# A chunk's last head pair placed behind its search, MLP steps over two ticks fewer, first products sorted

## The chip, the cores and the metric

The kernel runs on one NeuronCore of one Trainium2 chip, in one launch. Its engines are TensorE (PE; its weight loads are shown as PEld), VectorE (DVE), ScalarE (ACT), GpSimd (POOL) and SyncE (SP), which issues every DMA here. The metric is the device time of one execution in microseconds. Three runs of the kernel before gave 1281.82, 1284.70 and 1287.45 us.

## The reference

```python
# q, k, v: (4, 8, 576, 64)
scores = q @ k.T / 8
kth = the 32nd largest score of each row of 576
attn = softmax over the scores >= kth (the rest is masked)
x = (attn @ v) as 2304 tokens x 512
h = x @ w_in;  g = h - tanh(h);  x = g @ w_out           # MLP 0: 512 -> 2048 -> 512
h = x @ w_in;  g = h if h > 0 else exp(h) - 1;  out = g @ w_out   # MLP 1
```

All inputs are fp32.

## The kernel before, in words

The 2304 tokens are cut into six chunks of 384 rows (`CHUNKS`), numbered 0 to 5. A chunk has four head pairs (p = 0 to 3), and each pair two groups of three tiles of 128 query rows, so 48 groups in all (`groups`; `chunk_end[ci]` is the number of the first group behind chunk ci).

A group's attention: `scores` (PE matmuls `ps`, copied by ACT to `s`), then the search of the 32nd largest value on DVE, `topk_steps`: four rounds of MAX8 (L299) and three of MATCH_REPLACE8 (L313) for each tile, and a last pass (L320, or two on ACT) that makes the masked exponentials `e`. Then `transposed` brings `e` to the key side, in five blocks (PE `pt`, ACT copy `ph`). When a pair's second group is there, `norm` makes the reciprocal sums (`rt`, `rs`), `attend` multiplies by v (PE `av`, ACT copy `xun`), and `finish_pair` scales on POOL (L423) and splits the result into a high part `xh` (ACT) and a low part `xl` (POOL, L121 by way of `split`). `xh` and `xl` are the chunk's x, in four blocks of 128 of d_model, one for each pair.

A chunk's MLPs are 32 steps: (m, ft) with m = 0, 1 and ft = 0 to 15, 128 of d_ff each. `first` multiplies x by 128 columns of w_in: twelve matmuls (high x high, low x high, high x low, each over the four blocks kt) into `h`; `gate` applies the nonlinearity (DVE, some on POOL) and splits it into `gh`, `gl`; `second` adds nine matmuls into `acc`. Step i issues `first` and `gate` of step i + 1 ahead of its own `second`, so the last step of a chunk issues the first step of the next chunk, which needs all four pairs of that chunk. At the turn between a chunk's two MLPs, `between` copies `acc` (ACT `y`, three tiles), transposes it (PE `yt`, through the same three PSUM banks "at" that `ps`, `pt`, `av` and `rt` rotate through) and splits it into `zh` (ACT, L494) and `zl` (DVE, L495). `h` of the second MLP starts with the first two tiles of `zh` (`PARTED`).

In chunk 0 the weights come as fp32 words and are prepared on the chip (`prepare`: ACT L148, POOL L150, ACT L151, DVE L152, then `split` into `wp`) and written to DRAM; later chunks load them ready (`wt`). `load_next` runs at the end of each step.

The order is written by ticks, four to a group: a group's search runs in ticks t0 to t0 + 3, with t0 = 4 * g.at. Tables (`before`, `mid`, `late`, `ends`) put the other steps at ticks around it. The 32 steps of chunk ci are dealt evenly over the ticks from `starts[ci]` = 4 * chunk_end[ci] + `DONE[ci]` to `SPARE` = 3 ticks before `starts[ci + 1]`. Chunk 5's steps run behind the last tick. This written order is not the order on the engines: the tile framework's scheduler takes it as priorities and deals the instructions to the engines' queues by its own estimate of the time line, and each engine then runs its queue in order.

Chunk 0's last pair is "hurried" and has its own place in the loop; the change does not touch it.

Of the kernel before, what the change touches and what calls it, by code (L numbers as in the profile page):

```python
# [21 lines left out]
NPAIR = H // 2  # L22
# [50 lines left out]
FIRST_TICK = -8  # L73


SPARE = 3


NU = 384
# [8 lines left out]
def tile_topk_attention_two_mlps(  # L88
# [27 lines left out]
    def f(ap):  # L116
        return ap.bitcast(F32)
# [5 lines left out]
    def bank(tag, name, bufs):  # L123
        return ps.tile([P, 512], F32, tag=tag, name=name, bufs=bufs)
# [52 lines left out]
    units, groups, pair_units, pair_end, chunk_end = [], [], {}, {}, []  # L177
    x_tiles, xuns = {}, {}
    for ci, size in enumerate(SIZES):
        for p in range(NPAIR):  # L180
            row = []
            c0 = 0
            for b, q0, n in CHUNKS[ci]:
                for heads in ([[0], [1]] if n >= 256 else [[0, 1]]):
                    u = Unit()
# [17 lines left out]
            for us in cuts:  # L203
                g = Group()
# [11 lines left out]
    def hurried(u):  # L216

        return u.rush and u.last

    def load_q(u):  # L220
        u.qraw = sb.tile([P, NU], F32, tag="qraw", name=f"qraw{u.id}", bufs=QR_BUFS)
# [189 lines left out]
    def finish_pair(u):  # L411

        ci, p = u.ci, u.p
        n = SIZES[ci]
        if ci not in x_tiles:
            x_tiles[ci] = tuple(sb.tile([P, NPAIR, NMAX], F32R, tag=f"x{a}", name=f"x{a}{ci}") for a in "hl")
        xh, xl = (x[:, p, :n] for x in x_tiles[ci])
        xun, rs = xuns.pop((ci, p))[:, :n], u.rs[:, :n]
        if hurried(u):
            nc.scalar.activation(xh, xun, copy)  # L420
            nc.vector.tensor_sub(xl, xun, f(xh))
        else:
            nc.gpsimd.tensor_mul(xun, xun, rs)  # L423
            split(xh, xl, xun)
# [5 lines left out]
    def first(ci, m, ft):  # L430
        n = SIZES[ci]
        xh, xl = x_tiles[ci] if m == 0 else z_tiles[ci]
        h = bank("h", f"h{ci}_{m}_{ft}", 2)[:, :n]
        wv = weights.pop((ci, m, ft, 0)).rearrange("p a (k c) -> p a k c", c=P)
        jobs = [(wi, xs, kt) for wi, xs in ((0, xh), (1, xh), (0, xl)) for kt in range(4)]
        late = (n // P - 1) * P
        for cs in (slice(0, late), slice(late, n)) if m == 1 and ft < PARTED and late else (slice(0, n),):
            for a, (wi, xs, kt) in enumerate(jobs):
                nc.tensor.matmul(h[:, cs], wv[:, wi, kt], xs[:, kt, cs], start=(a == 0), stop=(a == len(jobs) - 1))  # L439
        t = sb.tile([P, NMAX], F32, tag="t", name=f"t{ci}_{m}_{ft}")[:, :n]  # L440
        if m == 0:
            nc.scalar.activation(t, h, AF.Tanh)
        else:
            nc.scalar.activation(t, h, AF.Relu, scale=-1.0)  # L444
            nc.scalar.activation(t, t, AF.Exp, scale=-1.0)  # L445
        parts[ci, m, ft] = h, t
# [94 lines left out]
    before, mid, late, ends = {}, {}, {}, {}  # L541

    def on(table, tick, do):
        table.setdefault(tick, []).append(do)

    for g in groups:
        t0 = 4 * g.at
        for u in g.units:
            lead = 6 if u.whole else 8
            on(before, max(-6, t0 - lead) if u.whole else t0 - lead, lambda u=u: (load_q(u), load_k(u)))  # L550
            on(before, t0 - 5, lambda u=u: split_qk(u))
            on(before, t0 + (1 if hurried(u) else 3), lambda u=u: load_v(u))
        for blk in range(NB):
            if not hurried(g.units[-1]):
                on(late, t0 + 4 + blk // 3, lambda g=g, blk=blk: transposed(g, blk))
        for j, (u, t) in enumerate(g.tiles):
            on(mid, t0 - 4 + j, lambda u=u, t=t: scores(u, t))
        for u in g.units:
            if hurried(u):
                continue  # L560
            if u.last:
                on(ends, t0 + 7, lambda u=u: norm(u.ci, u.p, u))
                on(ends, t0 + 7, lambda u=u: attend(u))
                on(ends, t0 + 7, lambda u=u: finish_pair(u))

    n_ticks = 4 * len(groups) + DONE[-1]
    starts = [4 * e + d for e, d in zip(chunk_end, DONE)]
    at_tick = {}
    for ci in range(len(SIZES) - 1):
        ticks = starts[ci + 1] - starts[ci] - SPARE  # L570
        for j in range(ticks):
            at_tick[starts[ci] + j] = range(ci * 2 * NF + 2 * NF * j // ticks, ci * 2 * NF + 2 * NF * (j + 1) // ticks)

    early = list(EARLY)
    for tick in range(FIRST_TICK, n_ticks):
# [8 lines left out]
        if tick == starts[0]:  # L584
            first(*steps[0])
            gate(*steps[0])
# [71 lines left out]
```

## Time and profile before

| what | value |
|---|---|
| median of three runs | 1284.7 us |
| the profiled execution's own time | 1284.19 us |
| its span, first to last instruction | 1282.4 us |
| PE busy | 1180.0 us (92%) |
| PE weight loads | 980.0 us (76%) |
| DVE busy | 991.0 us (77%) |
| ACT busy | 786.3 us (61%) |
| POOL busy | 605.8 us (47%) |
| mean granted TensorE clock | 0.966 |

Busy shares are means over stages that differ. Up to 164 us the attention of chunk 0 runs with the preparation of weights; from 164 to 393 us chunk 0's MLPs run beside chunk 1's search; from 393 to about 1088 us each chunk's MLPs run beside the next chunk's search; behind that only MLP steps are left. A matmul's end is modelled in the profile, and matmuls overlap, so the time from one start to the next says more than one's duration. In a timeline, the bracket at a row's end is the time for which the engine stood idle before it, and what ended that.

### The profile page before, as it was taken

The numbers are of one execution on the slowest core, as the hardware profiler recorded it, in microseconds if no ns is written. First come the engines' busy times: TensorE is split into PE (matmuls) and PEld (weight loads), VectorE is DVE, ScalarE is ACT, GpSimd is POOL, SyncE is SP. The second block draws the span as 40 slices with busy tenths as digits, with TensorE's granted clock in tenths as the row PEclk, the third lists the DMA queues.
The fourth block names the chain that finished last, engine by engine and source line by source line (L and its number), as shares of the span: only waits on it lengthen the run. The fifth ranks groups of instructions, "written<-read, shape, count | busy, mean of one in ns | idle before, by whom it ended". The sixth has DMA issues, their size and how long they took to land.

```text
span 1282.4 us, 19854 instructions
## 1 busy us (share of the span) xinstructions
PE 1180.0 (92%) x6424; PEld 980.0 (76%) x6424; DVE 991.0 (77%) x1951; ACT 786.3 (61%) x1716; POOL 605.8 (47%) x629
## 2 busy tenths in 40 slices
PE   4376889988989999999999999999999999999998
PEld 2233468867768878889888889878888988888896
DVE  7999999999899988698999598799598987100111
ACT  5787967787786555565656566566466655333333
POOL 4776558877995432334433344443333422233221
PEclk9975689999999999999999999999999999999999
DMA  7887437995769774777675778766676645677672
GB/s 229 266 279 246 130 97 242 317 316 189 238 237 357 238 230 150 231 234 236 210 232 172 224 231 268 227 212 198 212 232 232 209 157 187 209 253 262 211 248 75
DMA packets 97447, 286.13 MB, mean 223 GB/s; under 512 B 12096, under 2 KB 27968, under 8 KB 97344
## 3 DMA queue, kind: packets, MB, share of 16 engines
q1 hardware_dynamic: 97344, 284.87, 69.1%
q8 instruction: 51, 0.84, 0.3%
q14 instruction: 52, 0.43, 0.1%
HBM read 246.55 MB, written 38.27 MB: 222 GB/s over the span
## 4 chain that ended last, share of the span: by engine, by line
PE 71%; ACT 8%; DVE 8%; DMA 7%; issue 3%; POOL 2%; SPq 0%; POOLq 0%; ACTq 0%; DVEq 0%
PE h L439 28%; PE acc L475 27%; DMA wr<-in_w_dram 7%; PE av L359 6%; PE pt L341 4%; DVE vm L299 3%; PE ps L276 2%; DVE wf L152 2%; PE ps L277 2%; DVE w L313 2%; ACT wr L148 1%; POOL wr L150 1%; PE ps L274 1%; ACT s L278 1%; ACT e L316 1%
## 5 line engine op out<-in xcount | busy, mean ns | idle before, releaser
L121 POOL TENSOR_TENSOR gl<-g,gh 128x384 fp32r<-128x384 f32 x192 | 204.3, 1065 | 388.4 <-ACT gh L120 351.3
L299 DVE MAX8 vm<-w 128x8 f32<-128x576 f32 x432 | 316.1, 749 | 3.1
L475 PE MATMUL acc<-wt,gh 128*128 128x512 f32 x1008 | 271.6, 397 | 0.3 <-ACT gh L120 0.3
L313 DVE MATCH_REPLACE8 w<-vm,w 128x576 f32<-128x576 f32 x288 | 212.8, 740 | 0.0
L475 PEld LDWEIGHTS acc<-wt,gh 128*128 128x128 f32 x1008 | 184.9, 188 | 32.7 <-issue 2.1
L341 PE MATMUL pt<-ident,e 128*128 128x128 f32 (+1 forms) x720 | 121.0, 295 | 58.3 <-ACT e L316 41.7
L278 ACT ACTIVATE s<-ps 128x288 f32<-128x288 f32 (+1 forms) x320 | 124.2, 405 | 59.1 <-PE ps L277 51.6
L439 PE MATMUL h<-zh,wt 128*128 128x384 f32 (+2 forms) x768 | 149.4, 327 | 8.3 <-ACT zh L494 6.9
L299 DVE MAX8 vm<-s 128x8 f32<-128x576 f32 x144 | 107.9, 749 | 61.0 <-ACT s L278 60.2
L341 PEld LDWEIGHTS pt<-ident,e 128*128 128x128 f32 (+1 forms) x720 | 88.8, 143 | 86.5 <-ACT e L316 47.9
L120 ACT ACTIVATE gh<-g 128x384 fp32r<-128x384 f32 x192 | 100.5, 523 | 86.6 <-DVE g L453 39.7
L475 PE MATMUL acc<-wt,gl 128*128 128x512 f32 x504 | 151.1, 398 | 0.5 <-POOL gl L121 0.3
L453 DVE SCALAR_TENSOR_TENSOR g<-t,h 128x384 f32<-128x384 f32 x96 | 52.3, 545 | 118.8 <-ACT t L445 117.1
L439 PE MATMUL h<-xh,wt 128*128 128x384 f32 x672 | 140.6, 339 | 0.0
L439 PEld LDWEIGHTS h<-zh,wt 128*128 128x128 f32 x768 | 125.1, 190 | 19.9 <-ACT zh L494 8.5
L342 ACT ACTIVATE ph<-pt 128x384 f32<-128x384 f32 (+1 forms) x240 | 108.6, 489 | 34.9 <-PE pt L341 34.1
L439 PEld LDWEIGHTS h<-xh,wt 128*128 128x128 f32 x672 | 118.0, 188 | 7.2 <-issue 1.8
L320 DVE SCALAR_TENSOR_TENSOR e<-s,vm,e 128x576 f32<-128x576 f32 x115 | 110.4, 967 | 1.8 <-ACT e L303 0.8
L150 POOL TENSOR_TENSOR wr<-wr,tiny 128x512 f16<-128x512 f32 x64 | 89.7, 1408 | 37.7 <-ACT wr L148 37.2
L475 PEld LDWEIGHTS acc<-wt,gl 128*128 128x128 f32 x504 | 92.9, 188 | 18.8 <-POOL gl L121 1.2
L313 DVE MATCH_REPLACE8 w<-vm,s 128x576 f32<-128x576 f32 x144 | 106.5, 740 | 0.0
L444 ACT ACTIVATE t<-h 128x384 f32<-128x384 f32 x96 | 46.7, 488 | 94.5 <-PE h L439 94.2
(78 smaller groups left out, 2040.8 us busy)
## 6 DMA issues: line engine op xcount, KB each, us to landing
wt<-w SPq DMA_DIRECT2D x336, 512.0 KB, 4.3
wr<-in_w_dram SPq DMA_DIRECT2D x64, 512.0 KB, 5.0
w<-wp SPq DMA_DIRECT2D x64, 512.0 KB, 4.4
kraw<-in_kT_dram SPq DMA_DIRECT2D x120, 144.0 KB, 4.5
vraw<-in_vL_dram SPq DMA_DIRECT2D x64, 160.0 KB, 3.5
qraw<-in_qT_dram SPq DMA_DIRECT2D x88, 96.0 KB, 3.6
out_dram<-o SPq DMA_DIRECT2D x16, 256.0 KB, 5.1
out_dram<-o SPq DMA_DIRECT2D x4, 128.0 KB, 4.4
```

The lines of the kernel that those rows point to most:

```text
L120: nc.scalar.activation(hi, src, copy)
L121: nc.gpsimd.tensor_sub(lo, src, f(hi))
L150: nc.gpsimd.tensor_mul(top, scaled, tiny)
L278: nc.scalar.activation(s[lo:hi, cs], pt[lo:hi, :HS], copy)
L299: nc.vector.max(g.vm[:, j, min(r, 1)], u.s[t] if r == 0 else g.w[j])
L313: nc.vector.match_replace(g.w[j], v, u.s[t] if r == 0 else g.w[j], FILL)
L320: nc.vector.scalar_tensor_tensor(u.e[t], u.s[t], v[:, 7:8], u.e[t], op0=ALU.is_ge, op1=ALU.mult, accum_out=g.sum[:, j : j + 1])
L341: nc.tensor.transpose(pt[:kn, j * P : j * P + P], v.e[t][:, k0 : k0 + kn], ident)
L342: nc.scalar.activation(g.ph[:kn, blk, :nq], pt[:kn, :nq], copy)
L359: nc.tensor.matmul(pt[h * D : h * D + D, :n], v.vraw[h][:kn, blk], v.g.ph[:kn, blk, cs], start=(blk == 0), stop=(blk == NB - 1),)
L439: nc.tensor.matmul(h[:, cs], wv[:, wi, kt], xs[:, kt, cs], start=(a == 0), stop=(a == len(jobs) - 1))
L475: nc.tensor.matmul(acc[ci, m][:, t], gx[:, t * P : t * P + P], wt[:, wi], start=(ft == 0 and k == 0), stop=(ft == NF - 1 and k == 2),)
```

## The change

Three edits. The last group of each chunk's last pair (`quick`, chunks 1 to 5) has all five blocks transposed at tick t0 + 4 (before: three at t0 + 4 and two at t0 + 5), and its `norm`, `attend` and `finish_pair` stand at t0 + 5 (before t0 + 7). The steps of a chunk are dealt over two ticks fewer (`SPARE` 5 for 3), so 31 ticks for 33 in chunk 0 and 27 for 29 in chunks 1 to 4. And in the first step of a chunk (m = 0, ft = 0) the twelve products are sorted by block of d_model, so that the nine of pairs 0 to 2 come before the three of pair 3. No instruction is added or taken away on any engine.

```diff
--- before.py
+++ after.py
@@ -73,7 +73,9 @@
 FIRST_TICK = -8
 
 
-SPARE = 3
+SPARE = [5, 5, 5, 5, 5, 5]
+
+QUICK = 6
 
 
 NU = 384
@@ -217,6 +219,10 @@
 
         return u.rush and u.last
 
+    def quick(u):
+
+        return u.ci < QUICK and u.p == NPAIR - 1 and u.g.at == chunk_end[u.ci] - 1
+
     def load_q(u):
         u.qraw = sb.tile([P, NU], F32, tag="qraw", name=f"qraw{u.id}", bufs=QR_BUFS)
         src = qT[u.b, 2 * u.p + u.heads[0] : 2 * u.p + u.heads[-1] + 1, :, u.q0 : u.q0 + u.n].rearrange("h d s -> d h s")
@@ -433,6 +439,8 @@
         h = bank("h", f"h{ci}_{m}_{ft}", 2)[:, :n]
         wv = weights.pop((ci, m, ft, 0)).rearrange("p a (k c) -> p a k c", c=P)
         jobs = [(wi, xs, kt) for wi, xs in ((0, xh), (1, xh), (0, xl)) for kt in range(4)]
+        if m == 0 and ft == 0:
+            jobs.sort(key=lambda x: x[2])
         late = (n // P - 1) * P
         for cs in (slice(0, late), slice(late, n)) if m == 1 and ft < PARTED and late else (slice(0, n),):
             for a, (wi, xs, kt) in enumerate(jobs):
@@ -552,22 +560,22 @@
             on(before, t0 + (1 if hurried(u) else 3), lambda u=u: load_v(u))
         for blk in range(NB):
             if not hurried(g.units[-1]):
-                on(late, t0 + 4 + blk // 3, lambda g=g, blk=blk: transposed(g, blk))
+                on(late, t0 + 4 + (0 if quick(g.units[-1]) else blk // 3), lambda g=g, blk=blk: transposed(g, blk))
         for j, (u, t) in enumerate(g.tiles):
             on(mid, t0 - 4 + j, lambda u=u, t=t: scores(u, t))
         for u in g.units:
             if hurried(u):
                 continue
             if u.last:
-                on(ends, t0 + 7, lambda u=u: norm(u.ci, u.p, u))
-                on(ends, t0 + 7, lambda u=u: attend(u))
-                on(ends, t0 + 7, lambda u=u: finish_pair(u))
+                on(ends, t0 + (5 if quick(u) else 7), lambda u=u: norm(u.ci, u.p, u))
+                on(ends, t0 + (5 if quick(u) else 7), lambda u=u: attend(u))
+                on(ends, t0 + (5 if quick(u) else 7), lambda u=u: finish_pair(u))
 
     n_ticks = 4 * len(groups) + DONE[-1]
     starts = [4 * e + d for e, d in zip(chunk_end, DONE)]
     at_tick = {}
     for ci in range(len(SIZES) - 1):
-        ticks = starts[ci + 1] - starts[ci] - SPARE
+        ticks = starts[ci + 1] - starts[ci] - SPARE[ci]
         for j in range(ticks):
             at_tick[starts[ci] + j] = range(ci * 2 * NF + 2 * NF * j // ticks, ci * 2 * NF + 2 * NF * (j + 1) // ticks)
```

What the scheduler makes of it differs on every engine from 164 us on. Three places are shown; the number behind a name is a buffer's.

On ACT, at the turn of chunk 0 (`y0` are the copies of the first MLP's result, `zh0` the split that the second MLP waits for, `wr` and `wp` belong to the weights, the rest to chunk 1's attention). Before:

```order
L489 ACTIVATE y0_1_2790<-acc0_0_1612 128x512
L489 ACTIVATE y0_2_2791<-acc0_0_1612 128x512
L120 ACTIVATE wp1_5_1_2868<-wf1_5_1_2863 128x512
L342 ACTIVATE ph1_2_1_2_0_384_0_2762<-pt1_2_1_2_0_384_0_0_2763 128x384
L316 ACTIVATE e1_2_1_0_0_0_2872,sum1_2_1_2_1_0_0_2742<-e1_2_1_0_0_0_2872,b21_2_1_2_1_0_0_3058 128x576
L342 ACTIVATE ph1_2_1_2_0_384_0_2762<-pt1_2_1_2_0_384_0_1_2768 128x384
L342 ACTIVATE ph1_2_1_2_0_384_0_2762<-pt1_2_1_2_0_384_0_2_2773 128x384
L151 ACTIVATE wr1_6_1_2965<-wr1_6_1_2965 128x512
L494 ACTIVATE zh0_2787<-yt0_0_2793 128x4x128
L148 ACTIVATE wr1_7_0_3022<-wr1_7_0_3022 128x512
L494 ACTIVATE zh0_2787<-yt0_1_2801 128x4x128
L494 ACTIVATE zh0_2787<-yt0_2_2809 128x4x128
```

Now, from the first copy:

```order
L497 ACTIVATE y0_0_2699<-acc0_0_1574 128x512
L497 ACTIVATE y0_1_2700<-acc0_0_1574 128x512
L497 ACTIVATE y0_2_2701<-acc0_0_1574 128x512
L122 ACTIVATE wp1_5_1_2778<-wf1_5_1_2773 128x512
L502 ACTIVATE zh0_2697<-yt0_0_2703 128x4x128
L502 ACTIVATE zh0_2697<-yt0_1_2711 128x4x128
L502 ACTIVATE zh0_2697<-yt0_2_2719 128x4x128
L309 ACTIVATE e1_2_1_0_0_1_2939<-s1_2_1_0_0_1_2548,mb1_2_1_2_1_0_0_2835 128x576
L309 ACTIVATE e1_2_1_0_0_2_2940<-s1_2_1_0_0_2_2615,mb1_2_1_2_1_0_0_2835 128x576
L150 ACTIVATE wr1_6_1_2927<-wr1_6_1_2927 128x512
```

Seven instructions stood between the last `y0` and the first `zh0`, and one between the first and the second `zh0`; now one `wp` stands there.

On ACT, at the turn of chunk 1. Before:

```order
L489 ACTIVATE y1_0_5219<-acc1_0_4300 128x512
L489 ACTIVATE y1_1_5220<-acc1_0_4300 128x512
L489 ACTIVATE y1_2_5221<-acc1_0_4300 128x512
L303 ACTIVATE e2_3_1_192_0_0_5425<-s2_3_1_192_0_0_5082,mb2_3_2_3_1_192_0_5353 128x576
L303 ACTIVATE e2_3_1_192_0_1_5426<-s2_3_1_192_0_1_5153,mb2_3_2_3_1_192_0_5353 128x576
L303 ACTIVATE e2_3_1_192_0_2_5427<-s2_3_1_192_0_2_5197,mb2_3_2_3_1_192_0_5353 128x576
L494 ACTIVATE zh1_5217<-yt1_0_5223 128x4x128
L494 ACTIVATE zh1_5217<-yt1_1_5231 128x4x128
L494 ACTIVATE zh1_5217<-yt1_2_5239 128x4x128
```

Now:

```order
L497 ACTIVATE y1_0_5204<-acc1_0_4300 128x512
L497 ACTIVATE y1_1_5205<-acc1_0_4300 128x512
L497 ACTIVATE y1_2_5206<-acc1_0_4300 128x512
L284 ACTIVATE s2_3_1_192_0_1_5172<-ps2_3_1_192_0_1_1_0_5177 128x288
L348 ACTIVATE ph2_2_2_2_1_192_0_5133<-pt2_2_2_2_1_192_0_3_5183 128x384
L348 ACTIVATE ph2_2_2_2_1_192_0_5133<-pt2_2_2_2_1_192_0_4_5188 64x384
L502 ACTIVATE zh1_5202<-yt1_0_5208 128x4x128
L502 ACTIVATE zh1_5202<-yt1_1_5216 128x4x128
L502 ACTIVATE zh1_5202<-yt1_2_5224 128x4x128
L284 ACTIVATE s2_3_1_192_0_2_5301<-ps2_3_1_192_0_2_0_0_5302 128x288
```

Three exponentials (`e2_3`) stood ahead of `zh1`; now a score copy and two transposed blocks of chunk 2 stand there. The PE instructions that feed these three have moved behind the last `acc` with them.

On POOL, at the end of chunk 0's MLPs (`wp1_15_0` and `wp1_15_1` are the low halves of the last step's weights, `gl0_1_x` the low halves of the gates, `xun1_3`, `xl1` chunk 1's last pair, `qs2` and `kk2` low halves of chunk 2's q and k). Before:

```order
L301 TENSOR_SCALAR mb2_0_2_0_1_192_1_4095<-vm2_0_2_0_1_192_1_4094 128x3
L121 TENSOR_TENSOR gl0_1_13_3918<-g0_1_13_3915,gh0_1_13_3917 128x384
L121 TENSOR_TENSOR wp1_15_0_3729<-wf1_15_0_3724,wp1_15_0_3729 128x512
L423 TENSOR_TENSOR xun1_3_4060<-xun1_3_4060,rs1_3_4058 128x384
L121 TENSOR_TENSOR gl0_1_14_3978<-g0_1_14_3975,gh0_1_14_3977 128x384
L121 TENSOR_TENSOR wp1_15_1_3740<-wf1_15_1_3735,wp1_15_1_3740 128x512
L121 TENSOR_TENSOR xl1_2144<-xun1_3_4060,xh1_2143 128x384
L121 TENSOR_TENSOR gl0_1_15_4027<-g0_1_15_4024,gh0_1_15_4026 128x384
```

Now:

```order
L123 TENSOR_TENSOR gl0_1_13_3881<-g0_1_13_3878,gh0_1_13_3880 128x384
L123 TENSOR_TENSOR wp1_15_0_3714<-wf1_15_0_3709,wp1_15_0_3714 128x512
L123 TENSOR_TENSOR wp1_15_1_3725<-wf1_15_1_3720,wp1_15_1_3725 128x512
L123 TENSOR_TENSOR gl0_1_14_3963<-g0_1_14_3960,gh0_1_14_3962 128x384
L429 TENSOR_TENSOR xun1_3_3996<-xun1_3_3996,rs1_3_3994 128x384
L387 TENSOR_SCALAR r2_0_4477<-sum2_0_2_0_1_192_0_3844 128x3
L248 TENSOR_TENSOR qs2_1_1_192_1_4223<-qraw2_1_1_192_1_4131,qs2_1_1_192_1_4223 64x384
L123 TENSOR_TENSOR kk2_2_1_192_0_0_4433<-kraw2_2_1_192_0_0_4238,kk2_2_1_192_0_0_4433 128x576
L123 TENSOR_TENSOR xl1_2178<-xun1_3_3996,xh1_2177 128x384
L307 TENSOR_SCALAR mb2_0_2_0_1_192_1_4138<-vm2_0_2_0_1_192_1_4137 128x3
L123 TENSOR_TENSOR gl0_1_15_4054<-g0_1_15_4051,gh0_1_15_4053 128x384
```

The last `wp` has moved ahead of `gl0_1_14` and `xun1_3`; a `qs`, a `kk` and an `r` now stand between the scaling `xun1_3` and the low half `xl1`.

## Rows read from the trace of the kernel before

**Rows 1.** Windows: window, length, busy (PE, PEld, DVE, ACT, POOL), PEclk, DMA share, GB/s.

```profile
164.00:393.00 229.00, 206.53 (x1203) 171.17 (x1203) 219.38 (x399) 180.25 (x388) 184.66 (x176) 0.96 0.74 239
393.00:1088.00 695.00, 684.95 (x3973) 591.07 (x3971) 599.60 (x1230) 409.77 (x916) 263.69 (x288) 1.00 0.69 221
1088.00:1272.00 184.00, 182.61 (x943) 161.17 (x942) 20.21 (x36) 65.23 (x136) 51.66 (x51) 1.00 0.66 218
```

**Rows 2.** Waits of PE from 393 us on: us in total, times, longest.

```profile
PE h L439 <- ACT zh L494: 5.3, 5, 2.3
PE yt L492 <- ACT y L489: 2.2, 4, 0.7
```

**Rows 3.** Timeline of DVE, end of chunk 2's search: start, us, what [idle before].

```profile
527.05 0.82 DVE L320 SCALAR_TENSOR_TENSOR e<-s,vm,e 128x576 f32<-128x576 f32 x1
```

**Rows 4.** The timeline of PE where that group is first transposed.

```profile
555.04 0.82 PE L341 MATMUL pt<-ident,e 128*128 128x128 f32 x6
```

**Rows 5.** The timeline of PE at the turn of chunk 1.

```profile
490.78 1.63 PE L492 MATMUL yt<-ident,y 128*128 128x128 f32 x12 [0.69 <-ACT y L489]
494.71 1.67 PE L439 MATMUL h<-zh,wt 128*128 128x256 f32 x10 [2.30 <-ACT zh L494]
```

**Rows 6.** The timeline of ACT at the same turn.

```profile
490.13 1.57 ACT L489 ACTIVATE y<-acc 128x512 f32<-128x512 f32 x3 [0.19 <-PE acc L475]
...
493.57 1.58 ACT L494 ACTIVATE zh<-yt 128x512 fp32r<-128x512 f32 x3
```

**Rows 7.** The timeline of ACT at the turn of chunk 3.

```profile
863.21 0.86 ACT L342 ACTIVATE ph<-pt 128x384 f32<-128x384 f32 x2
...
865.62 1.56 ACT L494 ACTIVATE zh<-yt 128x512 fp32r<-128x512 f32 x3
```

**Rows 8.** The timeline of PE at the turn of chunk 3.

```profile
861.81 0.95 PE L341 MATMUL pt<-ident,e 128*128 128x128 f32 x6
```

**Rows 9.** The timeline of PE at the turn of chunk 2.

```profile
674.46 1.94 PE L492 MATMUL yt<-ident,y 128*128 128x128 f32 x12 [0.42 <-ACT y L489]
677.69 0.98 PE L439 MATMUL h<-zh,wt 128*128 128x256 f32 x6 [1.29 <-ACT zh L494]
```

**Rows 10.** The timeline of PE at the turn of chunk 0.

```profile
278.98 0.39 PE L475 MATMUL acc<-wt,gl 128*128 128x512 f32 x1
...
289.05 1.21 PE L439 MATMUL h<-zh,wt 128*128 128x256 f32 x8 [1.54 <-ACT zh L494]
```

**Rows 11.** The timeline of ACT at the same turn.

```profile
281.89 1.56 ACT L489 ACTIVATE y<-acc 128x512 f32<-128x512 f32 x3
283.32 0.65 ACT L120 ACTIVATE wp<-wf 128x512 fp32r<-128x512 f32 x1
...
288.42 1.07 ACT L494 ACTIVATE zh<-yt 128x512 fp32r<-128x512 f32 x2
```

**Rows 12.** The windows view of the 3.41 us behind chunk 1's turn.

```profile
495.77:499.18 3.41, 3.41 (x19) 3.41 (x17) 3.41 (x8) 0.41 (x1) 0.00 (x0) 0.50 0.00 0
```

**Rows 13.** The timeline of POOL at the last weight products of chunk 0.

```profile
388.07 1.31 POOL L121 TENSOR_TENSOR wp<-wf,wp 128x512 fp32r<-128x512 f32 x1
...
391.85 1.46 POOL L121 TENSOR_TENSOR gl<-g,gh 128x384 fp32r<-128x384 f32 x1
```

**Rows 14.** The timeline of PE at the last step of chunk 0.

```profile
391.69 0.86 PE L439 MATMUL h<-zh,wp 128*128 128x384 f32 x4
```

**Rows 15.** The timeline of PE where chunk 3's last pair is finished.

```profile
757.33 3.59 PE L359 MATMUL av<-ph,vraw 128*64 128x384 f32 x20
```

**Rows 16.** The timeline of ACT at the same place.

```profile
763.66 0.53 ACT L120 ACTIVATE xh<-xun 128x384 fp32r<-128x384 f32 x1 [0.21 <-POOL xun L423]
```

**Rows 17.** The timeline of POOL at the same place.

```profile
757.89 1.41 POOL L121 TENSOR_TENSOR kk<-kraw,kk 128x576 fp32r<-128x576 f32 x1
...
764.26 1.01 POOL L121 TENSOR_TENSOR xl<-xun,xh 128x384 fp32r<-128x384 f32 x1 [0.64 <-ACT xh L120]
```

**Rows 18.** Part 6 of the page, DMA issues: KB each, median us to landing.

```profile
kraw<-in_kT_dram SPq DMA_DIRECT2D x120, 144.0 KB, 4.5
```

## The prediction

> **What bounds the kernel now.** I read the windows view by stage first. From 393 us to the end of the search PE is busy for 684.95 of 695 us and DVE for 599.60; behind that PE for 182.61 of 184 us, with hardly anything beside it; from 164 to 393 us no engine is full: DVE 219.38 of 229, PE 206.53, POOL 184.66 [rows 1]. So from 393 us on a microsecond counts only if PE stands idle in it, and between 164 and 393 us there are 229 - 206.5 = 22.5 us of idle PE. The waits of PE come second. From 393 us on the first two rows are of one kind, the turn between a chunk's two MLPs: `h` waiting for `zh`, 5.3 us in five places, and `yt` for `y`, 2.2 us in four [rows 2]. No wait for a pair's `xh` or `xl`, and none for a weight load, is among the larger ones: at the start of a chunk, where two of the three edits aim, PE loses next to nothing today. Nor is the search late for PE: chunk 2's last group has its last `e` at 527.05 + 0.82 = 527.87 us, and PE transposes it at 555.04 us, 27 us later [rows 3, 4].
>
> The Trainium skill (Perfetto Trace Analysis, section Identifying the Most-Contended Engine) says that matmul busy time is a bad measure of headroom and that the weight loads' busy share should be taken. By that rule the middle stage is not full: its loads are busy for 591.07 / 695 = 85.0%, those of the last stage for 161.17 / 184 = 87.6% [rows 1], which would leave up to 2.6% of 695, or 18 us, for a better order to win. This is a rival with a small chance below; the sum does not use it.
>
> **The change part by part.** No instruction is added or removed, so all of it is order. I take the turns first, since the new queues differ most there, then what is left of the edits.
>
> Turn of chunk 1. PE waits 0.69 us ahead of `yt` and 2.30 us ahead of `h` [rows 5], 3.0 in all. ACT does the three `y` (from 0.19 us behind the last `acc`, 1.57 us), then three exponentials up to 493.57, and only then `zh`; `h` starts 494.71 - 493.57 = 1.14 us behind the first `zh` [rows 5, 6]. In the new queue a score copy and two `ph` stand in place of the exponentials. Two `ph` take 0.86 us [rows 7], one copy about half of that. From the last `acc` to `h`: 0.19 + 1.57 + 0.43 + 0.86 + 1.14 = 4.2 us. In it PE now has `yt` (1.63 [rows 5]), the six transposes (0.95 [rows 8]) and a score pair (an estimate of 0.3, a third of those six): 2.9 us. It waits 1.3 us: 1.7 us less than before.
>
> Turn of chunk 2: the waits before are 0.42 + 1.29, and 0.3 inside `yt`, which took 1.94 instead of 1.63 [rows 5, 9], so 2.0 us. The new queue has the same pattern as at chunk 1: 0.7 us less. Turn of chunk 3: two score copies and two q/k copies stood between the last `ph` (863.21 + 0.86 = 864.07) and `zh` (865.62 [rows 7]); they now stand behind it, so `zh` comes 1.55 us earlier, but two score pairs that covered the wait (0.5 by the estimate above) leave with them: 1.0 us less. Turn of chunk 4: of the 7.5 us of rows 2, chunks 1 to 3 have 3.0, 1.7 and about 1.1, which leaves some 0.85 each for chunks 4 and 5; with the pattern of chunk 1 it becomes 1.3, a loss of 0.4. Chunk 5's turn has the same order as before. Sum of turns 1 to 4: 1.7 + 0.7 + 1.0 - 0.4 = 3.0 us. From 393 us on this reaches the end whole, since PE is full on both sides. Bounds: 0, if other waits take their place, and 6, if the waits of chunks 1 to 3 went altogether.
>
> Turn of chunk 0. From the last `acc` (278.98 + 0.39) to `h` (289.05 [rows 10]) PE spends 9.7 us. Work in it: `yt` 1.63 and nine transposes (1.5 times the 0.95 of six, 1.4), so it waits 6.7 us. ACT has one `y` row, a `wp`, and then transposed blocks, masks and weight pieces before the last `zh` at 288.42 [rows 11]. In the new queue only one `wp` (0.65) stands between `y` and `zh`: 0.19 + 1.56 + 0.65 + 1.14 = 3.5 us, of which 1.63 is `yt`. It waits 1.9 us: 4.8 less.
>
> Of the clock: the granted TensorE clock is 0.50, the lower level (1.2 GHz), for 3.41 us right behind the wait at chunk 1's turn, while PE is busy for all of it [rows 12]. Work done at half rate for 3.41 us is 1.7 us lost. With a wait of 1.3 us in place of 3.0 I count this 1.7 as won. The bounds are 0 (the clock falls all the same) and 1.7, less another 1.7 if it falls at a turn where it does not now.
>
> What chunk 0's turn is worth at the end is less sure, because the steps behind it are fed by weights that are prepared just in time. The low half for the last step is ready at 388.07 + 1.31 = 389.38 [rows 13], and PE takes it at 391.69 [rows 14]: 2.3 us can pass without POOL being earlier. POOL is a little earlier in the new queue: the last `wp` no longer stands behind `gl0_1_14` (1.46 [rows 13]) and `xun1_3`. So the turn brings between 2.3 and 4.8 us, and nothing if the other waits among the 22.5 us grow by as much. I take 3.5, the middle.
>
> The denser deal itself moves the search back against the MLPs; the 27 us between search and transposes cover this, and without that cover each microsecond of lateness would be one of PE. The sort computes the same twelve products and finds no wait to fill. The earlier last pair finds none either, and it puts something new in POOL's queue: at the starts of chunks 1 to 3 a `qs` and a `kk` now stand between the scaling and `xl`. Today, at chunk 3, `av` ends at 757.33 + 3.59 = 760.92 [rows 15], `xh` is there at 764.19 [rows 16], 3.3 us later, and `xl` at 765.27 [rows 17], 4.35 later. In the new PE queue 24 matmuls stand between the last `av` and the first product with that `xh`, and ten more before the one with `xl`. At 684.95 / 3973 = 0.172 us each [rows 1] that is 4.1 and 5.8 us. `xh` has 0.8 us to spare; `xl` with a `kk` (1.41 [rows 17]) and a `qs` of no more than that ahead of it comes between 4.35 and 7.2 us. I count 0 (a `qs` and `kk` already copied when POOL gets there cost about what is spare); the bounds are 0 and 1.4 us for each of three chunks. SP's loads move with the steps that issue them; as no load is among PE's larger waits and DMA's share is 0.69 in the middle stage [rows 1], this is counted at nothing, with the price in the rival below.
>
> Sum: 3.0 + 1.7 + 3.5 = 8.2 us off the profiled execution's own 1284.2 us, so 1276.0. That execution lies 0.5 us under the median of 1284.7; the forecast is 0.7% below the median.
>
> **The rivals.** A: the gain at chunk 0's turn and of the clock is used up, because the stretch up to 393 us is held by the weight pieces that DVE, ACT and POOL pass to each other, and the wait comes back a few steps later. DVE's 219 of 229 us speak for it; the 2.3 us of slack against it. Then only the 3.0 us of turns 1 to 4 are left: 1281.2.
>
> B, slower: POOL runs in order, so a `kk` that waits for its load holds `xl`, and PE stops at the start of a chunk. It would be at chunks 1 to 3, the three with this order. A k load lands 4.5 us after its issue [rows 18]; issued as late as the old place of the last pair needed it, `xl` comes 4.5 us late, and the clock's half rate adds 1.7: 6.2 at each. With all three, 1284.2 - 8.2 + 18.6 = 1294.6; with two it is 1288.4, so it decides from three on. Against it: no such wait now, and q and k are issued eight ticks, two groups, ahead.
>
> C, more: the other waits between 164 and 393 us (22.5 - 6.7 = 15.8) also go by half, and chunk 0's turn brings its whole 4.8: 3.0 + 1.7 + 4.8 + 7.9 = 17.4, or 1266.8. The search's new order there is better or worse by chance, so nothing speaks for half rather than none. By the rule of the Trainium skill above, 1276.0 - 18 = 1258 would be the far end; I give that 0.03 of C's chance.
>
> D: the scheduler's new order does not show on the chip, since the engines are as full as before: 1284. The waits at the turns are rows of queue order, so this is unlikely; I put it in with A.
>
> **How the numbers follow.** Forecast (1276.0, own range 1270 to 1282) 0.52; A with D (1281 to 1284) 0.27; B 0.10; C 0.11. A difference of under 0.5%, 6.4 us, cannot be told from none here: faster means under 1278.3, slower over 1291.1. Faster: three quarters of the forecast's 0.52, and C's 0.11, and a little of A: 0.52. Slower: most of B, 0.08. Same: 0.40. The range reaches from C's 1267 to B with two chunks, 1288.
>
> **What would show it.** Right: PE's wait for `zh` at chunk 1's turn near 1 us and no half clock behind it; at chunk 0's turn 3 to 4 us from `acc` to `h` in place of 9.7; idle PE from 164 us to the start of chunk 1's MLPs some 3 to 5 us less than 22.5. A would show the same turns but a new wait of `h` or `acc` for `wp` or `gl` before chunk 1's first step. B would show PE waiting for POOL's `xl` in the first step of chunks 1 to 3. I am wrong if the time falls while the turns stay as they are, or if PE begins to wait for `e` from 393 us on.

## The result and the profile after

The changed kernel takes 1273.08 us (median of four runs, 1271.72 to 1273.84), the kernel before beside it 1283.29 us: ratio 0.9916, 95% interval 0.9893 to 0.9940. The forecast was 1276.0. Run again later (e9_again) it gave 1274.48, ratio 0.9929 (0.9909 to 0.9950). The profiled execution took 1273.46 us, 10.7 less than the 1284.2 of before.

The windows of the three stages; columns as in [rows 1]:

```profile
164.00:393.00 229.00, 209.24 (x1230) 174.21 (x1230) 220.84 (x401) 182.52 (x393) 186.31 (x176) 0.99 0.74 251
393.00:1088.00 695.00, 687.84 (x3981) 591.52 (x3980) 602.01 (x1224) 409.89 (x918) 267.18 (x286) 1.00 0.66 220
1088.00:1272.00 184.00, 176.52 (x907) 154.41 (x906) 19.10 (x34) 64.31 (x132) 50.69 (x50) 0.99 0.60 207
```

PE is busy 2.7 us more of the first window and its clock is 0.99 where it was 0.96; the last window now holds the kernel's end. The waits of PE from 393 us on (us in total, times, longest), which answer to [rows 2]:

```profile
PE yt L500 <- ACT s L284: 2.6, 3, 1.0
PE h L447 <- ACT zh L502: 1.4, 5, 0.3
...
PE yt L500 <- ACT ph L348: 0.7, 1, 0.7
PE yt L500 <- ACT y L497: 0.7, 1, 0.7
```

`h` waits 1.4 us for `zh` where it waited 5.3; `yt` now waits 3.3 us for PSUM banks that `s` and `ph` have still to empty, and 0.7 for `y`. Chunk 1's turn, PE and then ACT, in place of [rows 5, 6]:

```profile
480.89 1.53 PE L500 MATMUL yt<-ident,y 128*128 128x128 f32 x12 [1.04 <-ACT s L284]
482.72 2.15 PE L447 MATMUL h<-zh,wt 128*128 128x256 f32 x16 [0.30 <-ACT zh L502]
```

```profile
478.96 1.57 ACT L497 ACTIVATE y<-acc 128x512 f32<-128x512 f32 x3 [1.02 <-PE acc L483]
480.41 0.43 ACT L284 ACTIVATE s<-ps 128x288 f32<-128x288 f32 x1
480.70 0.86 ACT L348 ACTIVATE ph<-pt 128x384 f32<-128x384 f32 x2
481.58 1.58 ACT L502 ACTIVATE zh<-yt 128x512 fp32r<-128x512 f32 x3
```

And chunk 0's. What [rows 10] leave out of the kernel before, between the last `acc` and `h`:

```profile
280.13 0.55 PE L341 MATMUL pt<-ident,e 128*128 128x128 f32 x3 [0.43 <-ACT s L278]
282.06 0.55 PE L341 MATMUL pt<-ident,e 128*128 128x128 f32 x3 [1.38 <-ACT s L278]
284.41 3.10 PE L492 MATMUL yt<-ident,y 128*128 128x128 f32 x12 [1.81 <-ACT ph L342]
```

After, PE and then ACT, in place of [rows 10, 11]:

```profile
271.91 0.40 PE L483 MATMUL acc<-wt,gl 128*128 128x512 f32 x1
273.15 1.63 PE L500 MATMUL yt<-ident,y 128*128 128x128 f32 x12 [0.84 <-ACT y L497]
275.62 2.15 PE L447 MATMUL h<-zh,wt 128*128 128x256 f32 x16 [0.84 <-ACT zh L502]
```

```profile
271.93 0.68 ACT L122 ACTIVATE kk<-kraw 128x576 fp32r<-128x576 f32 x1 [0.40 <-DMA kraw<-in_kT_dram]
272.52 1.55 ACT L497 ACTIVATE y<-acc 128x512 f32<-128x512 f32 x3
273.95 0.64 ACT L122 ACTIVATE wp<-wf 128x512 fp32r<-128x512 f32 x1
274.47 1.58 ACT L502 ACTIVATE zh<-yt 128x512 fp32r<-128x512 f32 x3
```

From the last `acc` to `h` it is 275.62 - 272.31 = 3.3 us, where it was 9.7, and PE waits 1.7 us in it, where it waited 0.43 + 1.38 + 1.81 + 1.54 = 5.2.

The table gives four marks in PE's timeline for every kernel run: the start of the first and of the third `h` of chunk 0, the start of the third `h` of chunk 1, and the end of the last `acc`; "rest" is the last minus the third. Up to the first mark the order in the changed kernel is that of before; that mark lies anywhere from 159.9 to 164.1 us in these single traces. The kernel before has done 1.6 us more of PE's work by the third mark than the changed one (an estimate: six transposes and six score products, which start 0.11 and 0.15 us apart), and has that much less in the rest; four of the score products, 0.6 us, lie between the first and the third `h` of chunk 0. e4, e7, e10, e11 and e12 have the same work ahead of the mark as the changed kernel, and e4, e10, e11 and e12 also the same order up to there on every engine, so that six traces show what one order gives at the third mark: 394.1 to 396.7 us.

| kernel | median us | ratio to before | 1st h | 3rd h | 3rd h, chunk 1 | last acc | rest |
|---|---|---|---|---|---|---|---|
| before | 1283.1 to 1283.6 | 1 | 163.8 | 186.4 | 404.1 | 1277.2 | 873.1 |
| after | 1273.08 | 0.9916 | 161.4 | 180.6 | 395.0 | 1266.5 | 871.6 |
| e9_again | 1274.48 | 0.9929 | 162.2 | 182.1 | 396.7 | 1268.3 | 871.6 |
| e1_quick | 1289.68 | 1.0048 | 159.9 | 182.6 | 399.3 | 1280.7 | 881.4 |
| e2_no_sort | 1284.22 | 1.0006 | 161.3 | 184.0 | 405.4 | 1277.4 | 872.1 |
| e3_sort | 1280.37 | 0.9975 | 164.1 | 183.3 | 404.1 | 1275.4 | 871.3 |
| e4_deal_c0 | 1281.60 | 0.9975 | 162.3 | 181.6 | 395.5 | 1274.9 | 879.4 |
| e5_sort_c0 | 1276.33 | 0.9939 | 163.1 | 182.4 | 398.3 | 1271.9 | 873.6 |
| e6_sort_rest | 1283.17 | 1.0001 | 162.0 | 183.0 | 404.4 | 1276.6 | 872.2 |
| e7_deal_rest | 1279.62 | 0.9963 | 163.3 | 183.4 | 403.6 | 1276.2 | 872.6 |
| e8_fill | 1282.38 | 0.9993 | 163.4 | 184.0 | 402.6 | 1275.3 | 872.7 |
| e10_early | 1275.05 | 0.9937 | 161.7 | 181.8 | 394.1 | 1267.4 | 873.3 |
| e11_mix | 1278.18 | 0.9959 | 161.7 | 181.8 | 395.0 | 1270.8 | 875.8 |
| e12_spare4 | 1269.05 | 0.9890 | 162.9 | 182.1 | 394.1 | 1260.6 | 866.5 |

Of the changed kernel's 10.7 us, 9.2 are there by chunk 1's third `h`, and 1.5 come behind it.

### The profile page after: what moved, and what is told of

Same layout as the page of the kernel before. It is cut to its first block, busy times and chain, and to the rows that moved or that the text cites. A ratio compares the mean times of both kernels' runs of the same rounds, so it can differ in the third digit from the quotient of the medians.

```text
span 1271.7 us, 19863 instructions
## 1 busy us (share of the span) xinstructions
PE 1176.6 (93%) x6424; PEld 976.0 (77%) x6424; DVE 995.0 (78%) x1951; ACT 786.4 (62%) x1716; POOL 610.5 (48%) x629
## 4 chain that ended last, share of the span: by engine, by line
PE 68%; DVE 12%; DMA 9%; ACT 7%; issue 2%; POOL 2%; SPq 0%; POOLq 0%; ACTq 0%; DVEq 0%
PE h L447 27%; PE acc L483 27%; DMA wr<-in_w_dram 7%; PE av L365 6%; DVE vm L305 4%; PE pt L347 4%; DVE w L319 4%; DVE wf L154 2%; PE ps L282 2%; PE ps L283 2%; DVE e L326 1%; ACT wr L150 1%; POOL wr L152 1%; DMA wt<-w 1%; ACT ph L348 1%
## 5 line engine op out<-in xcount | busy, mean ns | idle before, releaser
L447 PEld LDWEIGHTS h<-xh,wt 128*128 128x128 f32 x672 | 117.9, 188 | 10.1 <-issue 1.8
L326 DVE SCALAR_TENSOR_TENSOR e<-s,vm,e 128x576 f32<-128x576 f32 x115 | 113.7, 997 | 1.3 <-ACT e L309 0.5
```

Of the source, the lines that this page charges most:

```text
L326: nc.vector.scalar_tensor_tensor(u.e[t], u.s[t], v[:, 7:8], u.e[t], op0=ALU.is_ge, op1=ALU.mult, accum_out=g.sum[:, j : j + 1])
```

## The experiments

The theory ahead of the first four was that the denser deal's order makes the gain, most of it at chunk 0's turn.

**e1_quick**: the early last pairs alone (`SPARE` 3 throughout, no sort).

```diff
-SPARE = [5, 5, 5, 5, 5, 5]
+SPARE = [3, 3, 3, 3, 3, 3]
-        if m == 0 and ft == 0:
-            jobs.sort(key=lambda x: x[2])
```

> The last pair of each chunk early, without the denser deal and without the sort. The turn of chunk 0 has the same ACT order as before. Theory (the gain is the denser deal's order, mostly at chunk 0): 1282 to 1286, no change, with acc to h of chunk 0's turn near 9.7 us. Rival 1 (the earlier last pair itself gains at the chunk starts): 1273 to 1277. Rival 2 (any new order of the search moves the time by some us, up or down, without a place that can be named): a time off 1284 by 4 us or more in either direction, with the turn of chunk 0 as before.

Measured: 1289.68 us, ratio 1.0048 (1.0031 to 1.0065), slower. The rest takes 881.4 us in place of 873.1; some 2.5 us of that is work that moved behind the mark (an estimate: seven `acc`, four score products and three transposes fewer ahead of it). By itself this edit is a loss. The theory and rival 1 had none; it fits rival 2, a new order that moves the time by some us either way, with chunk 0's turn as before (9.5 us).

**e2_no_sort**: the changed kernel without the sort (the last two lines of the diff above).

> The changed kernel with the products of a chunk's first step in their old order. Theory: 1272 to 1275, like the changed kernel, with the turn of chunk 0 near 3.5 us from acc to h. Rival 1 in the form that the sort gains at the chunk starts: 1277 or more. Rival 2: off 1273 by 4 us or more with the same turn.

Measured: 1284.22 us, ratio 1.0006 (0.9993 to 1.0019). The turn of chunk 0 is nearly as short as the theory wanted (280.4 to 284.6 us, 4.2 where 3.5 was expected), turns 1 to 3 are those of the changed kernel, chunk 4's waits 0.4 us longer, and nothing is won. The first theory fell here: the third mark lies 10.4 us later than in the changed kernel. Both rivals were left.

**e3_sort**: the sort alone, in the kernel before.

```diff
+        if m == 0 and ft == 0:
+            jobs.sort(key=lambda x: x[2])
```

> The kernel before with only the sort of a chunk's first twelve products. Theory: 1282 to 1286, no change, chunk 0's turn near 9.7 us. Rival 1 (the sort gains): 1280 or less with PE's gain in the first steps of chunks 1 to 5. Rival 2: off 1284 by 4 us or more.

Measured: 1280.37 us, ratio 0.9975 (0.9958 to 0.9992): 3.2 us faster, just short of the rival's 1280, and not the theory's "no change".

**e4_deal_c0**: the changed kernel with chunks 1 to 5 dealt as before.

```diff
-SPARE = [5, 5, 5, 5, 5, 5]
+SPARE = [5, 3, 3, 3, 3, 3]
```

> The changed kernel, but the denser deal only in chunk 0; chunks 1 to 4 are dealt as before. The ACT order at turn 0 is that of the changed kernel, at turns 1 to 4 nearly that of before. Theory by the prediction's terms: turn 0 is worth 3.5 us and, if the half clock behind turn 1 returns, turns 1 to 4 cost 3.0 + 1.7, so 1284 - 3.5 = 1280; by the marks of the changed kernel's trace (nearly all gained by chunk 1's first MLP): 1273 to 1276. Rival 1: 1273 (the deal does not matter). Rival 2: no place can be named, anything from 1270 to 1285.

Measured: 1281.60 us, ratio 0.9975 (0.9961 to 0.9988), nearest to the 1280 by the prediction's terms, and neither 1273 nor the 1273 to 1276 by the marks. The third mark is that of the changed kernel (395.5), the rest takes 7.8 us longer. ACT at chunk 1's turn:

```profile
480.39 1.58 ACT L497 ACTIVATE y<-acc 128x512 f32<-128x512 f32 x3 [0.92 <-PE acc L483]
481.84 0.73 ACT L284 ACTIVATE s<-ps 128x288 f32<-128x288 f32 x2
482.42 0.56 ACT L247 ACTIVATE qs<-qraw 128x384 fp32r<-128x384 f32 x1
482.84 0.71 ACT L122 ACTIVATE kk<-kraw 128x576 fp32r<-128x576 f32 x1
483.41 1.60 ACT L502 ACTIVATE zh<-yt 128x512 fp32r<-128x512 f32 x3
```

With the early last pairs and the old deal, q/k copies stand between `y` and `zh` at the turns of chunks 1 to 3; PE's wait of `h` for `zh` from 393 us on is 6.0 us here, 5.9 in e1_quick, 1.4 in the changed kernel. PE is idle for 14.6 us of the rest (9.2 in the changed kernel), 5.5 more, and half clock for 3.4 us behind chunk 1's turn costs 1.7: 7.2 of the 7.8. The two edits belong together: what one loses behind chunk 0 the other wins back, and no more than that, since e3_sort, with neither of them, has a rest of 871.3 us against the changed kernel's 871.6.

The second theory, for the next four, was that the denser deal gains in chunk 0 only with the sort ahead of it.

**e5_sort_c0** and **e6_sort_rest**: the sort in chunk 0 alone, and in chunks 1 to 5 alone.

```diff
-        if m == 0 and ft == 0:
+        if ci == 0 and m == 0 and ft == 0:
```

```diff
-        if m == 0 and ft == 0:
+        if ci > 0 and m == 0 and ft == 0:
```

> The changed kernel with the sort in chunk 0 alone. Theory now (the first theory fell with e2_no_sort: the denser deal gains only together with the sort, because the sorted products keep PE busy and its clock up at the end of chunk 0's search, and because the order that follows has no long wait ahead of chunk 0's turn): 1272 to 1276, like the changed kernel, with half clock in no stretch between 185 and 320 us. Rival 1 (the sort gains at the starts of chunks 1 to 5): 1281 to 1285. Rival 2 (an accident of one order): somewhere between, with waits at other places than either.

> The changed kernel with the sort in chunks 1 to 5 alone; PE's queue differs from the changed kernel's only in chunk 0. Theory now: 1282 to 1286, with the long wait of acc for gh and some 12 us of half clock between 270 and 290 us, as in e2_no_sort. Rival 1: 1272 to 1275.

Measured: 1276.33 us (0.9939, 0.9923 to 0.9955) and 1283.17 us (1.0001, 0.9986 to 1.0016). The first lies just above the theory's 1272 to 1276, the second inside its range. Without the sort in chunk 0 nothing is won; with it there alone, 7.2 of the 10 us. From chunk 1's third `h` on, e6_sort_rest runs 9.4 to 10.1 us behind the changed kernel to the end. PE in e6_sort_rest ahead of chunk 0's turn, and the window of its half clock:

```profile
271.88 1.22 PE L483 MATMUL acc<-wt,gh 128*128 128x512 f32 x2 [2.37 <-ACT gh L122]
275.86 0.80 PE L483 MATMUL acc<-wt,gl 128*128 128x512 f32 x1 [2.76 <-POOL gl L123]
...
279.91 2.82 PE L500 MATMUL yt<-ident,y 128*128 128x128 f32 x12 [0.69 <-ACT y L497]
282.93 3.01 PE L447 MATMUL h<-zh,wt 128*128 128x256 f32 x16 [0.21 <-ACT zh L502]
```

```profile
271.20:284.90 13.70, 9.36 (x30) 7.04 (x31) 13.16 (x25) 8.98 (x17) 9.03 (x11) 0.50 0.74 243
```

The turn is short (0.9 us of waiting), but the idle time has moved ahead of it, 5.1 us for `gh` and `gl`, and PE works for 9.4 us at 1.2 GHz.

In e5_sort_c0 the order up to 385 us is the changed kernel's, but the expectation on the clock was missed: half clock from 277.3 to 284.1 us. ACT there:

```profile
274.70 0.68 ACT L122 ACTIVATE kk<-kraw 128x576 fp32r<-128x576 f32 x1 [2.29 <-DMA kraw<-in_kT_dram]
275.29 1.55 ACT L497 ACTIVATE y<-acc 128x512 f32<-128x512 f32 x3
```

A k load, waited for 1.9 us longer than in the changed kernel (0.40), held `y`, and PE waited 2.7 us for that.

**e7_deal_rest**: the changed kernel with chunk 0 dealt as before.

```diff
-SPARE = [5, 5, 5, 5, 5, 5]
+SPARE = [3, 5, 5, 5, 5, 5]
```

> The changed kernel, but chunk 0 dealt as before; the turn of chunk 0 has nearly the order of before, turns 1 to 4 that of the changed kernel. Theory now (turn 0 is most of it, and needs the denser deal): the first step of chunk 0 as in the changed kernel (third h near 181 us), the turn of chunk 0 near 9 us from acc to h, 1279 to 1284. Rival (turns 1 to 4 are worth the 3.0 + 1.7 us of the prediction, the sort 3): 1275 to 1278.

Measured: 1279.62 us, ratio 0.9963 (0.9951 to 0.9976), as the theory had it, at the lower end of its range (the profiled execution took 1283.14, the second longest of twelve): from `acc` to `h` at chunk 0's turn 9.2 us, and from chunk 1's third `h` on 8.6 to 9.7 us behind the changed kernel.

**e8_fill**: e2_no_sort with PE kept busy near chunk 0's turn by 24 transposes of no use.

```diff
+        if ci == 0 and m == 1 and ft == 0:
+            for _ in range(24):
+                nc.tensor.transpose(h[:, :P], ident, ident)
```

> e2_no_sort with 24 more transposes of the identity into the bank of the first h of chunk 0's second MLP, which the first product there overwrites; nothing waits for their result, and they stand in PE's queue around the last acc of chunk 0, where e2_no_sort waits for gh and gl and has half clock. They cost PE 24 x 0.14 = 3.3 us where it is idle anyway. Theory (PE's idle time is what lets the clock fall): half clock between 265 and 290 us mostly gone, 3 to 6 us less than e2_no_sort: 1278 to 1281. Rival (the clock falls for another reason, or they delay what is behind them): 1284 to 1288.

Measured: 1282.38 us, ratio 0.9993 (0.9976 to 1.0010), just above the theory's range; the interval overlaps that of e2_no_sort (0.9993 to 1.0019), so a gain at the end is not shown. The same window in e2_no_sort and in e8_fill:

```profile
272.00:289.10 17.10, 11.93 (x47) 9.38 (x49) 17.10 (x33) 10.33 (x19) 10.54 (x12) 0.50 0.80 266
```

```profile
272.00:289.10 17.10, 11.95 (x87) 9.61 (x87) 17.06 (x30) 10.84 (x20) 9.69 (x12) 0.90 0.76 246
```

PE is as busy in both, but the clock is 0.90 in place of 0.50 and 87 matmuls go through in place of 47. The dummies cost PE some 2.6 us (24 at 0.11 us each; 3.3 expected) and stood where `acc` had waited 3.2 us for `gh`; that wait is gone too, so order and clock changed together. Little of it reaches the end: `rt` then waits 3.7 us for `zl` of DVE, which is busy for 17.06 of these 17.1 us.

**e9_again**: the changed kernel once more, unedited.

> The changed kernel once more. In e5_sort_c0 the queues up to 385 us are those of the changed kernel, and yet ACT waited 2.3 us for a k load ahead of y at chunk 0's turn (0.4 in the changed kernel's trace) and PE had half clock there. If that wait is luck of one execution: 1272 to 1274 again, in every run, and no half clock at chunk 0's turn in this profile or at most a short one. If the first four runs were lucky: 1275 to 1278.

Measured: 1274.48 us (1273.28 to 1277.19, six runs). Neither expectation quite: the first runs lay at the lower end of a wider spread. Half clock came for 3.4 us ahead of the turn (270.8 to 274.2), none behind it.

**e10_early**: sort everywhere, denser deal in chunk 0 alone, early last pair in chunk 1 alone (chunk 0's has its own place).

```diff
-SPARE = [5, 5, 5, 5, 5, 5]
+SPARE = [5, 3, 3, 3, 3, 3]
-QUICK = 6
+QUICK = 2
```

> The sort everywhere, the early last pair in chunks 0 and 1, the denser deal in chunk 0; behind chunk 1 the order is that of e3_sort (nearly that of before). Theory (the gain is made before 395 us; behind it the early last pairs cost what the denser deal then wins back): 1272 to 1275, like the changed kernel, though the turns of chunks 1 to 4 have the order of before. The prediction's terms (turns 1 to 4 worth 3.0, the clock 1.7): 1276 to 1279.

Measured: 1275.05 us, ratio 0.9937 (0.9916 to 0.9959), at the upper end of the theory's range and 1 us under that of the prediction's terms. Its rest is 873.3 us, the changed kernel's 871.6: what the change does behind chunk 1's third `h` is worth 1.7 us here, and what comes ahead of it the remainder. Turns 2 to 4 wait as before; chunk 1's, with 1.95 us, less than the 3.0 of before.

**e11_mix** and **e12_spare4**: the first has chunks 2 and 4 dealt as before and the last pairs of chunks 3 and 5 late again; the second deals the steps over one tick fewer in place of two.

```diff
-SPARE = [5, 5, 5, 5, 5, 5]
+SPARE = [5, 5, 3, 5, 3, 3]
-QUICK = 6
+QUICK = (0, 1, 2, 4)
-        return u.ci < QUICK and
+        return u.ci in QUICK and
```

```diff
-SPARE = [5, 5, 5, 5, 5, 5]
+SPARE = [4, 4, 4, 4, 4, 4]
```

> The changed kernel with chunks 2 and 4 dealt as before and chunk 3's and 5's last pair late again, by the marks of the traces so far the better order for each chunk. Theory: 1271 to 1273, 1 to 2 us under the changed kernel; if the marks mislead (each order brings its own waits): 1274 or more.

> The changed kernel with steps dealt over one tick fewer than before, in place of two. At the turns of chunks 1, 2 and 4 nothing stands between y and zh in ACT's queue. If the turns set the time behind 395 us: 1 to 3 us under the changed kernel, 1270 to 1272. Theory (a turn has a floor of y, transposes and zh; what leaves it comes back elsewhere): 1273 to 1277, turn 0 as in the changed kernel.

Measured: e11_mix 1278.18 us (0.9959, 0.9946 to 0.9971), a miss: marks of one order don't add up to those of a mixture. e12_spare4 1269.05 us (1267.58 to 1272.77), ratio 0.9890 (0.9868 to 0.9911): below both expectations (1270 to 1272, 1273 to 1277). It beats both kernels, the changed one in e9_again by 5.4 us. Its waits of PE from 393 us on:

```profile
PE yt L500 <- ACT y L497: 2.8, 4, 0.7
PE h L447 <- ACT zh L502: 1.5, 5, 0.3
...
PE yt L500 <- ACT s L284: 0.5, 1, 0.5
```

That is 4.8 us at the turns against 5.4 in the changed kernel, so the turns give 0.6 of the 5.1 us by which its rest is shorter. The stretch from chunk 1's third `h` on, in the changed kernel and in e12_spare4:

```profile
395.00:1272.00 877.00, 862.36 (x4874) 744.19 (x4873) 619.11 (x1253) 473.28 (x1047) 317.87 (x336) 1.00 0.65 217
```

```profile
394.10:1266.00 871.90, 858.38 (x4875) 743.64 (x4873) 617.76 (x1253) 473.93 (x1047) 315.55 (x336) 1.00 0.69 218
```

4.0 us are PE's busy time, with the same number of matmuls at the same clock. In part the traces tell what costs it: the 400 `av` products of this stretch keep PE busy for 64.09 us in the changed kernel and for 61.51 in e12_spare4. Most `av` start in twos, some 6 ns apart, with 0.32 us from one two to the next; some start alone and take 0.32 us each. In the changed kernel 24 of the 400 start alone, in e12_spare4 14; ten that run singly in place of five twos are 5 x 0.32 = 1.6 us (an estimate). What costs the remainder of the 4.0 stays open, and no run changed the order of the `av` by itself.

## Why the prediction was right, point by point

**The turns: right to a few tenths.** Chunk 1's turn was to wait 1.3 us, and waits 1.04 + 0.30; chunk 2's has the same pattern and the same numbers. Chunk 3 waits 1.8 us where it waited 2.65 (0.85 won, 1.0 said); chunk 4's 0.98 is 0.1 more than before, where I had feared a loss of 0.4. Together that is 2.9 us of waiting less, 3.0 said. Chunk 0's waits 0.84 + 0.84 = 1.7 us, 1.9 said; but the 6.7 us that I took for its wait before were 5.2, because `yt` ran at the lower clock there (3.10 us for 1.63; half clock from 284.1 to 287.6). What waits at turns 1 and 2 is not what I named: `yt` stands for a PSUM bank that a score copy empties, rather than `h` for `zh`.

**The half clock behind chunk 1's turn: gone, as said.** In place of [rows 12]:

```profile
482.70:486.10 3.40, 3.38 (x29) 3.38 (x29) 3.37 (x7) 0.87 (x2) 0.00 (x0) 1.00 0.00 0
```

That the shorter wait did this is not shown. e10_early and e4_deal_c0 have the same order up to 544 us, and the same waits at this turn (0.17 + 0.62 + 1.16 us); `h` behind it, in e10_early and then in e4_deal_c0:

```profile
483.15 2.15 PE L447 MATMUL h<-zh,wt 128*128 128x256 f32 x16 [1.16 <-ACT zh L502]
484.58 3.53 PE L447 MATMUL h<-zh,wt 128*128 128x256 f32 x16 [1.16 <-ACT zh L502]
```

The first ran at full clock, the second at half (484.9 to 488.3 us). At the turns that wait 1.4 us or less no trace has half clock from chunk 1 on, but of the 1.7 us that I counted as won, an unknown part belongs to the one profiled execution of before.

**What the turns are worth: too large.** "From 393 us on this reaches the end whole" was the step. e10_early, which has the same work ahead of chunk 1's third `h` and nearly the old turns behind it, is idle there for 12.1 us, the changed kernel for 9.2: 2.9 us, as in the forecast. But the rest is only 1.7 us shorter, since PE's busy time is 1.2 us longer. Against e3_sort, which also has nearly the old turns (and two score products, 0.3 us, fewer in its rest), it is not shorter at all: 2.5 us less idle, and 2.4 more busy for the same work. A wait that goes is won whole; an order that also changes how long PE is busy isn't. The marks say 3.1 where I had 4.7 (873.1 to 871.6, and the 1.6 that had moved there), and 1.7 of that is the half clock of the one trace of before. At chunk 0's turn, from its third `h` to chunk 1's, 217.8 us became 214.4: 3.4, and 2.4 without the 1.0 of work that moved, where I had 3.5 and 2.3 as the least. PE's idle time there fell by the same 2.4 (18.6 to 16.1). From 164 us to the start of chunk 1's MLPs it fell by 2.7 (22.5 to 19.8), where 3 to 5 was to be the sign that I am right: waits elsewhere took back part of the turn's.

**What was set at nothing and was not: the sort.** The sentence that failed is "The sort computes the same twelve products and finds no wait to fill". I had looked for that wait at the starts of chunks 1 to 5 and overlooked chunk 0, whose first step stands at the end of a search that PE waits for. Ahead of the last group's transposes PE could run six products before and runs twelve now; the wait that ends there is 1.24 us instead of 1.76. The pair's `av` just behind, before and after:

```profile
169.09 4.76 PE L359 MATMUL av<-ph,vraw 128*64 128x384 f32 x18
```

```profile
166.26 3.59 PE L365 MATMUL av<-ph,vraw 128*64 128x384 f32 x18
```

Before, PE had the lower clock from 164.7 to 171.5 us; after, none there. From the first to the third `h` of chunk 0 it is 19.2 to 20.1 us in all nine traces with this sort, and 20.6 to 22.7 in the five without: 3.4 us in the profiled pair, of which 0.6 is the four score products that moved. Of the other 2.8 the idle time gives only 0.3 (3.9 to 3.6 us); the remainder is busy time, most of it the clock's. And the clock is not the sort's alone: four of the nine traces with the sort, e9_again among them, have half clock for 3.4 us at the same place, and so have four of the five without. Between these it is 19.8 to 20.1 against 20.6 to 22.7 us, so the sort gives 0.5 to 2.9 us here, the moved work included, and the clock of one execution may give the rest. The start of chunk 0 itself gave another 2.4 that no part of the change explains, since the order up to there is the same (1.5 in e9_again). So the parts are 2.4 + 2.8 + 2.4 + 3.1 = 10.7, where the sum was 0 + 0 + 3.5 + 4.7 = 8.2: two terms at two thirds of their size, made up for by one that I had at 0 and by spread. That the total came out so near was in part luck.

**The terms were not independent.** e2_no_sort and e6_sort_rest have the turns that the sum counts and win nothing: chunk 0's old waits are gone, but some 5 us of new ones, of `acc` for `gh` and `gl`, stand ahead of the turn, with half clock behind them. That is rival A's mechanism, with the place ahead of the turn rather than behind it; in the changed kernel itself it was not seen (PE waits 1.3 us for POOL's `gl` from 164 to 393 us, 2.0 before). The sort, which I priced at nothing, decided whether some 10 us or none were won. Its larger part is not at the first step: from chunk 0's third `h` to chunk 1's it is 221.4 us in e2_no_sort and e6_sort_rest, 220.7 and 220.2 with the sort and the old deal (e3_sort, e7_deal_rest), and 214.4 with both. So the forecast held because sort and denser deal were there together. Whether it needed the earlier last pair is open, as no run has the other two edits without it.

**Rival B** (POOL's `xl` behind `qs` and `kk`) was not seen. Chunk 3, in place of [rows 15 to 17], POOL and then PE:

```profile
755.20 1.01 POOL L429 TENSOR_TENSOR xun<-xun,rs 128x384 f32<-128x384 f32 x1 [3.72 <-ACT xun L376]
756.69 1.02 POOL L248 TENSOR_TENSOR qs<-qraw,qs 64x384 fp32r<-64x384 f32 x1 [0.48 <-ACT qs L247]
...
758.00 1.43 POOL L123 TENSOR_TENSOR kk<-kraw,kk 128x576 fp32r<-128x576 f32 x1
759.38 1.03 POOL L123 TENSOR_TENSOR xl<-xun,xh 128x384 fp32r<-128x384 f32 x1
```

```profile
750.97 3.59 PE L365 MATMUL av<-ph,vraw 128*64 128x384 f32 x20
...
760.00 1.07 PE L447 MATMUL h<-xl,wt 128*128 128x384 f32 x5
```

`qs` and `kk` do stand ahead of `xl`, which is there 760.41 - 754.56 = 5.9 us behind `av` (4.35 to 7.2 said); PE needs it about then and shows no wait for it. A k copy that holds what stands behind it did occur, on ACT at chunk 0's turn in e5_sort_c0.

**Rival C** had half a mechanism right (other waits and the clock of chunk 0's stage), but PE's idle time from chunk 0's third `h` to chunk 1's fell only from 18.6 to 16.1 us. The Trainium skill's rule behind its far end (Perfetto Trace Analysis, section Identifying the Most-Contended Engine), that matmul busy time is a bad measure of headroom, is borne out in one place: e12_spare4 wins 4 us of PE's busy time in a stage that is busy for 862.4 of 871.6 us (the weight loads' busy time hardly differs, 744.2 and 743.6). The 18 us were not reached by any order here.

## What to carry to other kernels

Where a scheduler makes the order, price edits of order together: the earlier last pair gave +6 us alone and about 0 with the denser deal, the sort alone gave -3, and all three gave -10; an edit set at "nothing" can be the condition of the others. Look for what it fills at every place where it acts, the first chunk above all, where engines still wait. Near a turn, count the idle time ahead of it too, since a short turn that comes from late inputs is no gain. And try the neighbouring setting: one tick fewer was worth 5.4 us more than two.

## What the runs showed of the hardware

- Behind a stretch of waits PE's granted clock fell to 0.50 (1.2 GHz): in e6_sort_rest for 13.7 us, which begin within a wait of 2.4 us and hold one of 2.8; in e5_sort_c0 for 6.8 us, behind one of 2.7; the changed kernel waited 0.84 + 0.84 us at the same place and kept 1.00. So a wait can be paid for twice, the second time in the work behind it.
- It need not be: with the same waits at a turn, `h` behind it ran at half clock in one trace and at full clock in another (e4_deal_c0 and e10_early at chunk 1's turn; e1_quick and e4_deal_c0 at chunk 4's, 3.54 and 2.15 us for sixteen `h` behind 0.69 + 2.30 us). One trace of each kernel doesn't settle what a wait costs in clock.
- Two executions of one order differed by 1.7 us at 395 us, where loads and the clock have their say, and six traces of that order by up to 2.6 (394.1 to 396.7); from there to the end the two agree to 0.1 us (both 871.6).
- Two `av` products (form 128*64) mostly started 6 ns apart and took the time of one: from one such two to the next it was 0.32 us, as from one that stood alone to the next (at 514.9 to 515.5 us in the changed kernel).
